# The head of a one-core attention and MLP block: x0 in two halves on two queues, another order of loads and products

## The chip, the cores and the metric

The kernel runs on one core of a Trainium2 chip. The time is device microseconds of one execution on that core; the median of three runs stands for a kernel. TensorE (PE) multiplies, VectorE (DVE), ScalarE (ACT) and GpSimd (POOL) work on its results, and SyncE (SP), ScalarE and GpSimd issue transfers.

## The reference

```python
xn = _layernorm(x, axis=-1)          # x: 1 x 2048 x 640, bf16
# A: linear attention, 32 heads of 20
q, k, v = split(xn @ wqkv)
pq, pk = phi(q), phi(k)              # phi(t) = (t + 1 if t > 0 else exp(t)) + 1e-6
kv = einsum("bhsd,bhse->bhde", pk, v)
z = einsum("bhsd->bhd", pk)
s = (pq @ kv / (pq . z + 1e-6)) @ wo
# B: MLP, 640 -> 1728 -> 640
g = silu(relu(xn @ w1) @ w2)
return x + s * g
```

## The kernel before, in words

The 2048 rows are 16 tiles of 128 rows (x0 to x15), four tiles to a chunk of 512 columns when turned. The columns of x, 640, are five blocks of 128.

The head: tiles of x are loaded (`x_load`), their means and variances taken (`bn`, `aggr`, `mean_act` on ScalarE, `half_mean_dve`), and the first four tiles are centred (`centre`), turned on PE (`head_turn`, the products on `ident` of L706), copied out of PSUM by VectorE or ScalarE (`xcT_copy`, L716 and L718), and multiplied with the key weight `wk` (`K_mm`, L733; `wk_load`, L585). Tiles are also normalised (`LN_norm`, L673) and turned a second way, by transposing transfers on SP's queue (`xnT_dma`, L722), for everything else. `fill(n)` (L605) issues idle products into a PSUM bank that nobody reads; `fill(32)` is eight of 512 columns.

The rest: the first MLP product, the query product and the others are units of seven products instead of eight on 2x2 blocks. `a0.s5` is step 5 of the first such unit of the MLP (`h_unit`, products at L1164), `p`, `q`, `k`, `m` and `g` are other families, `u` the second MLP product and `o` the attention's output. The operands of steps 5, 6, 7 and 4 are sums and differences of blocks, made on VectorE by `tt` (L936). The sums of the first chunks are `T0` (function `h_T`): number 1 (into `regE`), 3, 2 (into `regX`), 4 and 5. A step is a word of the string `PROGRAM`. `w1_load` (L582) brings 256 columns of w1, `w2_load` (L1059 and L1064) pieces of w2, `wo_load` (L1513) those of wo. `wv0`, `wv1` load the value weight (L567, on ScalarE's queue), `kv0`, `kv1` are its products (L1603), `W0` to `W5` join them with wo (L1629) and store the pieces (L1644). The denominators go out (`do`, L915) and come back spread (`rc`, L924) for the divisions (`dv`, L929). Last come `e`, `f` and `l`, the pieces of the last tiles.

The order is set by `Sched.place`: the words are recorded as operations in the order of `PROGRAM`. PE and SP keep that order always; the other engines keep it up to the word `|` (end of the head) and after it take, among the next 60 operations whose inputs are ready in a model of the times, the one with the earliest due time. The model's costs (`cost`, and in `_record` for transfers) decide only orders. Buffers hold more than one thing in turn, so loads wait until the former reader is done: w2 stands where w1 was, the value weight where scratch values of the units were.

Of the kernel before, what the change touches and what calls it, by code (L numbers as in the profile page):

```python
# [343 lines left out]


PROGRAM = """
lx0 lx2 ax1 ba0 mh0 ma0 lk02 lx3 lk24 ce0 lx4 ma1 ce1 lx5 lk45 lx7 lw2 tr0 pf3 cd0 lx6 bb0 ma2 sq1
ce2 cd1 ma3 tr1 k001 lw5 cd2 k012 ba3 lw3 ca3 mh3 ag0 ce3 S4 tr2 k102 S5 ca4 k023 k123 k134 ca5 k201
lw0 N1 tr3 N4 sq2 k213 S7 ca6 k035 ca7 k145 N5 ke0 k235 S6 bb3 N7 ag3 k301 k312 kr0 ke1 kr1 F1
N6 k325 ke2 P4 N0 kr2 P11 P5 F0 ke3 P10 KT5 kr3 KT4 N2 N3 |  # L350
SH0_1 F2 lx8 lq SH0_2 F3 lw6 wb KT7 KT6 xb wa SQ S8 xa n8 H110 n12 F6 H14 a0.s1 rb n11 F7
SM F4 SH0_3 xc T0 SH0_4 n13 H15 SK a0.s5 a0.s6 a0.s2 n9 H111 a0.s7 p1.s1 a0.s3 p1.s5 a0.s4 SH1 p1.s6 n10 n14 n15
y0 p1.s2 m0.s1 m0.s5 p1.s3 m0.s6 p1.s7 m0.s2 y4 y3 m0.s7 p1.s4 m0.s3 Kb8 m0.s4 a1.s5 a1.s1 F5 y2 Ka12 p0.s1 y1 p0.s5 a1.s6
a1.s2 p0.s6 a1.s7 a1.s3 y7 Ka8 a1.s4 p0.s2 a2.s5 a2.s1 y8 p0.s3 p0.s7 a2.s6 y5 y6 hh0 Ka11 T1 a2.s7 p0.s4 a2.s2 a2.s4 a2.s3
k1.s1 k1.s5 b0.s1 Kb12 b0.s5 y12 k1.s6 b0.s6 b0.s2 k1.s7 k1.s2 b0.s7 k1.s3 k1.s4 Kb15 b0.s4 q0.s1 b0.s3 y13 q0.s5 b1.s1 q0.s6 b1.s5 q0.s2
b1.s6 q0.s7 q0.s3 Kb11 q0.s4 b1.s7 k2.s5 b1.s3 k2.s1 b1.s4 y9 b1.s2 a3.s5 y11 k2.s6 a3.s1 Ka15 mv6 k2.s3 k2.s7 y14 a3.s6 a3.s2 k2.s4
y15 k2.s2 y10 a3.s7 q1.s5 q1.s1 a3.s3 w2a a3.s4 q1.s6 GS0 q1.s2 b2.s5 zm b2.s1 q1.s7 q1.s3 b2.s6 b2.s2 q1.s4 b2.s7 SH2 zs c0
b2.s4 m1.s1 GT1 b2.s3 GT2 m1.s5 b3.s1 m1.s6 m1.s2 b3.s5 b3.s6 m1.s7 m1.s3 b3.s2 ZS b3.s7 b3.s3 m1.s4 c1 b5.s1 b3.s4 b5.s5 b4.s5 b5.s6
b4.s1 b5.s2 b5.s7 sl b4.s6 b5.s3 zc w2b b5.s4 b4.s7 b4.s3 g0.s1 g0.s5 b4.s4 g0.s6 b4.s2 GT3 w2c dn hh1 w2d GT4 wo g0.s3
GS1 g1.s1 do0 g1.s5 g0.s2 g1.s6 g0.s7 rc0 g1.s7 do1 g1.s2 dv0 g1.s3 g1.s4 wv1 uSa0 uT1 g0.s4 uT3 wv0 uT2 uSb0 u0.s1 u0.s5  # L360
kv1 do2 kv0 rc1 W5 u0.s6 uT4 W4 u0.s2 W1 u0.s7 uSa1 W3 u0.s3 uSa2 uSb2 W0 u1.s1 u0.s4 W2 uSb1 u1.s5 u1.s6 u2.s5
u2.s1 u1.s2 u1.s7 oT u2.s6 u1.s3 u1.s4 oS0 u2.s2 xre o0.s1 u2.s7 uSa4 o0.s5 o0.s6 u2.s3 do3 u2.s4 o0.s7 o0.s2 oS1 o0.s3 uSa3 u4.s1
uSb3 dv1 uSb4 u4.s5 u4.s6 u4.s2 o0.s4 u4.s7 o1.s5 o1.s1 u4.s3 u4.s4 uSa6 rc2 o1.s6 u3.s5 oS2 u3.s1 o1.s2 o1.s7 rc3 dv2 o1.s3 u3.s6
uSb6 o1.s4 u3.s2 o2.s1 oS3 u3.s7 uSa5 o2.s5 o2.s6 u3.s3 u3.s4 o2.s2 o2.s3 o2.s7 oS4 u5.s1 u5.s5 o2.s4 u5.s6 o3.s1 u5.s2 o3.s5 uSb5 o3.s6
u5.s7 u5.s3 o3.s2 o3.s7 o3.s3 u5.s4 dv3 o3.s4 o4.s5 e3 o4.s1 u6.s1 u6.s5 o4.s6 u6.s6 uSa7 o4.s2 o4.s7 o4.s3 oS6 u6.s7 o4.s4 u6.s3 o5.s1
oS5 o5.s5 u6.s4 o6.s5 o5.s6 u6.s2 o6.s1 o5.s2 o5.s7 o5.s3 e0 uSb7 o5.s4 o6.s6 u7.s5 u7.s1 o6.s7 o6.s2 o6.s3 u7.s6 u7.s2 f0 o6.s4 u7.s7
u7.s3 f3 e1 f1 u7.s4 l0 l1
"""


def bass_recurrent_scan__linear_attn_block__dense_activation_relu__prompt_kernel(
# [187 lines left out]

    def x_load(t, n=1, E="SP", extra=()):  # L560
        sl = xs(t)
        dma(E, lambda eng: eng.dma_start(xin[:, sl:sl + n, :],
                                         x2[P * t:P * (t + n), :].rearrange("(t p) n -> p t n", p=P)),
            W=[("xin", sl + i) for i in range(n)], extra=extra)
# [106 lines left out]
    def LN_norm(t):  # L671
        mean, key = (msum[:, t, 1:2], ("msum", t, 1)) if t in BY_ACT else (mv[:, t, 0:1], ("mv", t))
        norms.append(sc.op("DVE", lambda eng: eng.tensor_scalar(  # L673
            out=xn[:, t, :], in0=xin[:, xs(t), :], scalar1=mean, scalar2=rsy[:, t:t + 1],
            op0=ALU.subtract, op1=ALU.mult), R=[("xin", xs(t)), key, ("rsy", t)], W=[("xn", t)]))
# [7 lines left out]
    def mean_act(t, lo):  # L683
        junk = ek[:, eks(t), 0, 0:D - lo]
        sc.op("ACT", lambda eng: eng.activation(out=junk, in_=xin[:, xs(t), lo:D], func=ACTF.Copy, scale=1.0 / D,
                                                accum_out=msum[:, t, 1:2]),
              R=[("xin", xs(t))], W=[("msum", t, 1), ("ek_e", eks(t))])
        sc.allow_unread.add(("ek_e", eks(t)))

    def centre(t):  # L690
        split = ((0, P * TS), (P * TS, D)) if t == 0 else ((0, D),)
        for part, (c0, c1) in enumerate(split):
# [5 lines left out]
            else:  # L698
                sc.op("DVE", lambda eng, c0=c0, c1=c1: eng.tensor_scalar(
                    out=xn[:, t, c0:c1], in0=xin[:, t, c0:c1], scalar1=msum[:, t, 0:1], scalar2=msum[:, t, 1:2],  # L700
                    op0=ALU.subtract, op1=ALU.subtract), R=[("xin", t), ("msum", t, 0), ("msum", t, 1)], W=[key])
# [1280 lines left out]
```

## Time and profile before

| | |
|---|---|
| runs | 202.53, 202.6, 204.0 us; median 202.6 |
| profiled execution | 202.56 us, span 201.3 us |
| PE | busy 197.2 us, 1312 products |
| DVE, ACT, POOL | busy 173.2, 132.5, 37.7 us |
| HBM read, written | 15.81 MB, 5.24 MB |

The span runs from the first to the last instruction that the profiler recorded; 1.26 us of the execution lie around it. A row of the timeline gives start, duration, engine, line, operation, output and inputs, count, and in brackets the idle time before it with what ended it. Modelled ends of products overlap, so that a group's length is a little over its count times the pitch. Line numbers are those of the kernel before; the changed one has them 6 or 7 higher.

### The profile page before, as it was taken

Reading aid. Unit: us, or ns where it says so; the run is one execution under the profiler, and the core shown is the slowest. Engines: PE = TensorE matmul, PEld = TensorE weight load, DVE = VectorE, ACT = ScalarE, POOL = GpSimd, SP = SyncE. Lnnn points to the kernel's source line nnn. Section 1 sums busy time; section 2 is a strip of 40 time slices with the busy share of each in tenths; the row PEclk is TensorE's granted clock in tenths of the full one; section 3 lists DMA queues with packets and bytes.
Section 4 is the critical chain, followed back from the end, with each engine's and each line's share of the span. In section 5 each row is a group of like instructions: output and inputs, shape, how many; then the busy total and the mean of one; then the engine's idle time right before and its main releaser. Section 6 shows DMA issues by size and latency. Waiting matters only on the chain.

```text
span 201.3 us, 3641 instructions
## 1 busy us (share of the span) xinstructions
PE 197.2 (98%) x1312; PEld 120.1 (60%) x1312; DVE 173.2 (86%) x407; ACT 132.5 (66%) x280; POOL 37.7 (19%) x66
## 2 busy tenths in 40 slices
...
PEclk9999999999999999999999999999999999999999
...
GB/s 179 335 259 95 150 351 144 70 98 109 108 145 134 150 256 174 171 99 67 113 17 118 270 264 184 295 212 148 355 185 72 258 65 36 33 67 65 36 65 98
DMA packets 38455, 30.43 MB, mean 151 GB/s; under 512 B 13733, under 2 KB 38437, under 8 KB 38437
## 3 DMA queue, kind: packets, MB, share of 16 engines
...
q8 instruction: 10, 0.16, 0.4%
q14 instruction: 8, 0.07, 0.1%
HBM read 15.81 MB, written 5.24 MB: 105 GB/s over the span
## 4 chain that ended last, share of the span: by engine, by line
PE 90%; DVE 4%; DMA 2%; ACT 1%; issue 1%; DVEq 0%
PE psT L991 43%; PE psT L1164 32%; PE psT L733 6%; PE psT L1494 2%; PE psT L823 2%; DMA reg<-reg 1%; ACT regE L743 1%; PE psT L1838 1%; DMA reg<-in_A_x_dram 1%; PE psT L841 1%; PE psT L1629 1%; PE psT L1603 1%; DVE stats L637 1%; DVE regX L936 1%; PE psT L895 1%
## 5 line engine op out<-in xcount | busy, mean ns | idle before, releaser
L1164 PE MATMUL psT<-reg 128*128 128x512 bf16 (+2 forms) x166 | 45.0, 370 | 0.0
L991 PE MATMUL psT<-reg,regH 128*128 128x320 bf16 (+1 forms) x224 | 35.0, 299 | 0.0
L991 PE MATMUL psT<-reg 128*128 128x320 bf16 (+1 forms) x178 | 28.4, 299 | 0.0
L991 PEld LDWEIGHTS psT<-reg,regH 128*128 128x128 bf16 (+1 forms) x224 | 21.9, 98 | 8.5
L1164 PEld LDWEIGHTS psT<-reg 128*128 128x128 bf16 (+1 forms) x166 | 15.9, 98 | 16.9 <-DVE regH L1217 0.6
L863 POOL DMA_DIRECT2D regH<-reg x16 | 18.6, 1188 | 20.9 <-DMA regH<-reg 9.4
L991 PEld LDWEIGHTS psT<-reg 128*128 128x128 f16 (+1 forms) x178 | 17.3, 98 | 7.4 <-DVE regE L899 0.4
L936 DVE TENSOR_TENSOR reg<-reg 128x1024 f16<-128x1024 bf16 (+11 forms) x30 | 19.0, 646 | 2.2 <-PE psT L991 1.8
L998 ACT ACTIVATE reg<-psT 128x320 f32<-128x320 f32 (+1 forms) x24 | 10.5, 436 | 15.8 <-PE psT L991 14.8
L1214 ACT ACTIVATE regH<-psT 128x512 bf16<-128x512 f32 (+1 forms) x24 | 14.6, 612 | 5.8 <-PE psT L1164 5.3
L1665 ACT ACTIVATE wv_sb<-psT 128x320 bf16<-128x320 f32 (+2 forms) x23 | 9.6, 424 | 11.4 <-PE psT L991 11.0
L991 PE MATMUL psT<-reg,pqT 128*128 128x320 bf16 (+1 forms) x84 | 15.8, 299 | 0.0
L936 DVE TENSOR_TENSOR psT<-psT,reg 128x320 f32<-128x320 f32 (+1 forms) x21 | 11.4, 543 | 2.8 <-PE psT L991 2.8
L637 DVE BATCH_NORM_STATS2 stats<-reg 128x6 f32<-128x320 bf16 x28 | 12.3, 480 | 1.4 <-DMA reg<-in_A_x_dram 1.1
L1853 ACT ACTIVATE reg<-psT 128x640 bf16<-128x640 f32 (+1 forms) x14 | 8.0, 570 | 7.5 <-PE psT L991 7.5
L733 PE MATMUL psT<-reg 128*128 128x320 bf16 x80 | 12.3, 299 | 0.0
L936 DVE TENSOR_TENSOR reg<-psT,reg 128x320 bf16<-128x320 f32 (+1 forms) x16 | 7.8, 489 | 5.1 <-PE psT L991 5.1
L1171 ACT ACTIVATE psT<-psT 128x512 f32<-128x512 f32 (+1 forms) x18 | 10.6, 594 | 1.8 <-PE psT L1164 1.7
L800 ACT ACTIVATE regE<-psT 128x512 bf16<-128x512 f32 x16 | 9.5, 603 | 2.6 <-PE psT L1164 2.5
L998 ACT ACTIVATE psT<-psT 128x320 f32<-128x320 f32 x17 | 7.2, 425 | 5.6 <-PE psT L991 5.5
L936 DVE TENSOR_TENSOR reg<-reg,wv_sb 128x640 bf16<-128x640 bf16 (+1 forms) x15 | 6.8, 456 | 4.3 <-ACT reg L1853 3.5
L733 PEld LDWEIGHTS psT<-reg 128*128 128x128 bf16 x80 | 7.7, 98 | 4.5 <-issue 0.4
...
## 6 DMA issues: line engine op xcount, KB each, us to landing
regH<-reg POOLq DMA_DIRECT2D x16, 320.0 KB, 3.8
reg<-in_B_w_dram SPq DMA_DIRECT2D x12, 320.0 KB, 4.9
scr<-rden SPq DMA_DIRECT2D x4, 640.0 KB, 7.0
reg<-in_A_x_dram SPq DMA_DIRECT2D x4, 640.0 KB, 6.1
...
regE<-scr SPq DMA_DIRECT2D x3, 640.0 KB, 6.1
reg<-in_A_x_dram SPq DMA_DIRECT2D x4, 320.0 KB, 4.8
...
```

The costliest lines, as they stand in the source:

```text
L637: sc.op("DVE", lambda eng: eng.bn_stats(stats[:, t, a, :], xv[:, HN * a:HN * (a + 1)]), R=[("xin", xs(t))], W=[("stats", t, a)])
L733: fns.append(lambda eng, a=a, k=k, lhs=lhs: eng.matmul(ps[bk[a]][:, 0:HN], lhsT=lhs, rhs=wk[:, k, HN * a:HN * (a + 1)], start=(k == 0), st ...
L800: exps.append(sc.op("ACT", lambda eng: eng.activation(out=e_, in_=src, func=ACTF.Exp), R=[key], W=[("er_e", es)]))
L863: dma("POOL", lambda eng: eng.dma_start(zacc[a], src, **kw), R=[key] + after, W=[("zacc", a)], chain=zchain[a])
L936: sc.op("DVE", lambda eng: eng.tensor_tensor(out=out, in0=in0, in1=in1, op=op), R=R, W=W, extra=extra)
L991: sc.group("PE", [(lambda eng, k=k, lhs=lhs, rhs=rhs: eng.matmul(ps[b][:, 0:HN], lhsT=lhs, rhs=rhs, start=(start and k == 0), stop=(k == n ...
L998: sc.op("ACT", lambda eng: eng.activation(out=dst, in_=ps[b][:, 0:HN], func=ACTF.Copy), R=[("ps", b)], W=[dkey], extra=extra)
L1164: sc.group("PE", [(lambda eng, k=k, lhs=lhs, rhs=rhs: eng.matmul(ps[b][:, 0:nn], lhsT=lhs if tile is None else rhs, rhs=rhs if tile is Non ...
L1171: sc.op("ACT", lambda eng: eng.activation(out=dst[:, 0:nn], in_=ps[b][:, 0:nn], func=ACTF.Copy), R=[("ps", b)], W=[dkey], extra=extra)
L1214: sc.op("ACT", lambda eng: eng.activation(out=dst, in_=ps[b], func=ACTF.Relu), R=[("ps", b)], W=[("hT", j, f)], extra=ex)
L1665: sc.op("ACT", lambda eng, lo=lo, hi=hi: eng.activation(out=g[:, lo:hi], in_=src[:, lo - HN * n:hi - HN * n], func=ACTF.Silu), R=[key, ("s ...
L1853: sc.op("ACT", lambda eng: eng.activation(out=o_[:, 0:n].rearrange("p (a n) -> p a n", a=2) if n == D else o_[:, 0:n], in_=src, func=ACTF. ...
```

## The change

x0 comes as two transfers of 128x320, the left half by SP's queue and the right half by ScalarE's; whoever reads the right half or the whole tile waits for both. x1 and x2 both come by ScalarE's queue (before: x1 alone). The key weight comes in five pieces of one block each, the first two directly behind x0 on SP's queue. `fill(29)` is seven idle products of 512 columns and one of 128. Five w1 pieces instead of four stand ahead of the transposing transfers on SP's queue (`wa` is the one that moved). The transposing transfers go in the order of tiles 1, 5, 4, 7, 6, 2, 0, 3; before 1, 4, 5, 7, 6, 0, 2, 3. The string `PROGRAM` is new from end to end; two constants of the model of transfers are edited.

```diff
 # Sched._record: model of a transfer
+            if names[1] == "in_A_x_dram" and size < 1e5:
+                lag, o.occ = -0.4, 0.1 if E == "ACT" else 0.5
 # Sched.place
-        lags = [(4.1, 0.6), (18.2, 1.2)]
+        lags = [(5.6, 0.6), (18.2, 1.2)]
 # PROGRAM, its first line
-lx0 lx2 ax1 ba0 mh0 ma0 lk02 lx3 lk24 ce0 lx4 ma1 ce1 lx5 lk45 lx7 lw2 tr0 pf3 cd0 lx6 bb0 ma2 sq1
+lx0 ba0 ax1 ax2 ma0 ma1 mh0 lk01 ce0 lk12 bb0 ma2 lx3 lk23 lk45 lk34 lx5 lx4 lx6 lw5 lx7 ce1 ag0 tr0
...
 # x_load
+        if t == 0:
+            for a, (Eh, key) in enumerate((("SP", ("xin", 0)), ("ACT", ("xin", 0, 1)))):
+                dma(Eh, lambda eng, a=a: eng.dma_start(xin[:, 0, HN * a:HN * (a + 1)], x2[0:P, HN * a:HN * (a + 1)]), W=[key])
+            return
...
-    fill(32)
+    fill(29)
...
 # bn, LN_norm, mean_act and centre: reads of x0's right half
-              R=[("xin", xs(t))], W=[("stats", t, a)])
+              R=[("xin", xs(t))] + ([("xin", 0, 1)] if t == 0 and a == 1 else []), W=[("stats", t, a)])
...
-              R=[("xin", xs(t))], W=[("msum", t, 1), ("ek_e", eks(t))])
+              R=[("xin", 0, 1) if t == 0 else ("xin", xs(t))], W=[("msum", t, 1), ("ek_e", eks(t))])
```

SP's queue from its start to the transposing transfers, before and after (`in_A_x` is x, `in_A_wqkv` the key weight here, `in_B_w` w1):

```order
L562 DMA reg<-in_A_x_dram 128x640 x2
L586 DMA reg<-in_A_wqkv_dram 128x2x640
L562 DMA reg<-in_A_x_dram 128x640
L586 DMA reg<-in_A_wqkv_dram 128x2x640
L562 DMA reg<-in_A_x_dram 128x640 x2
L586 DMA reg<-in_A_wqkv_dram 128x640
L562 DMA reg<-in_A_x_dram 128x640
L582 DMA reg<-in_B_w_dram 128x5x256
L562 DMA reg<-in_A_x_dram 128x640
L582 DMA reg<-in_B_w_dram 128x5x256 x3
L722 DMA_TRANSPOSE reg<-reg 128x5x128 x8
```

```order
L566 DMA reg<-in_A_x_dram 128x320
L592 DMA reg<-in_A_wqkv_dram 128x640 x2
L568 DMA reg<-in_A_x_dram 128x640
L592 DMA reg<-in_A_wqkv_dram 128x640 x3
L568 DMA reg<-in_A_x_dram 128x640 x3
L588 DMA reg<-in_B_w_dram 128x5x256
L568 DMA reg<-in_A_x_dram 128x640
L588 DMA reg<-in_B_w_dram 128x5x256 x4
L729 DMA_TRANSPOSE reg<-reg 128x5x128 x8
```

Half of x0 and x2 left this queue; the weight's first two pieces moved up behind x0, and a fifth w1 piece stands ahead of the transposing transfers.

PE and then VectorE at the first unit of the MLP, before (four fences: PE before, PE after, VectorE before, VectorE after; regE,pqT is step 5, regX,pqT step 6, regX,reg step 7, L823 and L830 plain MLP products; on VectorE, 128x1024 are the sums T0):

```order
L823 MATMUL psT<-reg 128x512 x10
L1164 MATMUL psT<-reg 128x512 x2
L823 MATMUL psT<-reg 128x512 x5
L1164 MATMUL psT<-regE,pqT 128x512 x2
L1164 MATMUL psT<-regX,pqT 128x512 x2
L1164 MATMUL psT<-reg 128x512 x3
L823 MATMUL psT<-reg 128x512 x5
L1164 MATMUL psT<-regX,reg 128x512 x2
```

```order
L830 MATMUL psT<-reg 128x512 x10
L1171 MATMUL psT<-reg 128x512 x2
L1171 MATMUL psT<-regE,pqT 128x512 x2
L830 MATMUL psT<-reg 128x512 x5
L1171 MATMUL psT<-regX,pqT 128x512 x2
L830 MATMUL psT<-reg 128x512 x5
L1171 MATMUL psT<-reg 128x512 x3
L1171 MATMUL psT<-regX,reg 128x512 x2
```

```order
L936 TENSOR_TENSOR regH<-reg 128x512
L936 TENSOR_TENSOR regX<-reg 128x1024
L936 TENSOR_TENSOR regE<-reg 128x1024
L936 TENSOR_TENSOR regX<-regX,reg 128x1024
L936 TENSOR_TENSOR reg<-reg 128x512
L759 TENSOR_SCALAR regE<-regE 128x640
L936 TENSOR_TENSOR regE<-reg,regX 128x1024
```

```order
L943 TENSOR_TENSOR regE<-reg 128x1024
L943 TENSOR_TENSOR regX<-reg 128x1024
L766 TENSOR_SCALAR regE<-regE 128x640
L943 TENSOR_TENSOR regX<-regX,reg 128x1024
L768 TENSOR_TENSOR reg<-regE 128x640
L943 TENSOR_TENSOR regE<-reg,regX 128x1024
```

Step 5 moved ahead of a group of plain products on PE, and the sum into regE that it needs moved to the front on VectorE.

SP's queue in the body, from w2 to the first load of x for the end (`rden` and `scr` are the denominators, L1644 and L1651 the stores of W), before and after:

```order
L1059 DMA reg<-in_B_w_dram 128x2x640 x6
L1059 DMA reg<-in_B_w_dram 128x640
L1064 DMA reg<-in_B_w_dram 64x640 x2
L1513 DMA reg<-in_A_wo_dram 128x640 x6
L915 DMA scr<-rden 640x1x512
L924 DMA reg<-scr 128x5x512
L915 DMA scr<-rden 640x1x512 x2
L924 DMA regE<-scr 128x5x512
L1644 DMA reg<-reg 40x640
```

```order
L1066 DMA reg<-in_B_w_dram 128x2x640 x2
L1520 DMA reg<-in_A_wo_dram 128x640 x6
L1066 DMA reg<-in_B_w_dram 128x640
L1071 DMA reg<-in_B_w_dram 64x640 x2
L1066 DMA reg<-in_B_w_dram 128x2x640 x4
L922 DMA scr<-rden 640x1x512
L931 DMA reg<-scr 128x5x512
L922 DMA scr<-rden 640x1x512
L1651 DMA reg<-reg 40x640
...
L1651 DMA reg<-reg 120x640
L931 DMA regE<-scr 128x5x512
```

Four of the w2 pieces moved behind wo, and the load of the second spread denominators moved behind the ten stores of W.

More of the change, by code (lines that the diff above doesn't have):

```diff
@@ L353 @@
[L353 to L364, printed above, removed]
@@ new lines @@
+ca5 k123 ce3 S5 k201 k035 tr3 ca6 N1 S4 N5 ca7 k213 ke0 k235 k135 k301 kr0 ke2 S7 ke1 k314 N4 S6
+k345 N7 ag3 kr1 P10 N6 N2 N0 P4 P11 N3 lq lx8 kr2 lw6 xb SH0_1 F1 ke3 kr3 |
+xa P5 KT5 wb S8 F2 F0 SH0_3 n8 F3 KT4 KT7 SH0_2 n12 SQ SK KT6 H111 rb H110 n11 a0.s1 F7 xc
+T0 F4 n10 F5 SM a0.s5 n9 n13 H14 F6 a0.s6 SH0_4 n15 n14 y6 H15 a0.s2 y0 a0.s7 p1.s1 a0.s3 T1 p1.s5 SH1
+a0.s4 p1.s6 p1.s2 y4 m0.s1 m0.s5 p1.s3 m0.s6 p1.s7 y2 m0.s2 m0.s7 y3 p1.s4 m0.s3 y7 Kb8 m0.s4 a1.s5 a1.s1 Ka12 p0.s1 y5 p0.s5
+a1.s6 y1 a1.s2 p0.s6 a1.s7 a1.s3 Ka8 a1.s4 p0.s2 y8 p0.s7 a2.s1 ZS a2.s5 hh0 a2.s6 Kb11 p0.s3 a2.s7 p0.s4 a2.s3 a2.s4 a2.s2 b0.s1
@@ new lines @@
+b0.s5 k1.s1 k1.s5 Kb12 y12 k1.s6 b0.s6 b0.s2 k1.s7 k1.s3 b0.s7 k1.s2 k1.s4 b0.s3 y13 b0.s4 q0.s1 q0.s5 Kb15 b1.s1 q0.s6 b1.s5 q0.s2 y9
+b1.s6 q0.s7 q0.s3 Ka11 y11 q0.s4 b1.s7 b1.s3 k2.s5 k2.s1 b1.s4 b1.s2 k2.s6 Ka15 a3.s1 a3.s5 k2.s7 k2.s2 a3.s6 y15 k2.s3 k2.s4 y14 a3.s2
+y10 GS0 a3.s7 q1.s5 q1.s1 a3.s3 a3.s4 GT3 q1.s6 q1.s2 zm b2.s5 GT1 b2.s1 GT2 q1.s7 q1.s3 b2.s6 b2.s2 q1.s4 b2.s7 SH2 zs c0
+b2.s4 m1.s1 b2.s3 m1.s5 b3.s1 m1.s6 b3.s5 m1.s2 b3.s6 m1.s3 m1.s7 c1 m1.s4 b3.s7 b3.s3 b5.s1 b5.s5 b3.s4 b5.s6 b3.s2 b4.s5 b4.s1 b5.s7 b5.s3
@@ new lines @@
+zc b4.s6 b5.s4 b5.s2 b4.s7 b4.s2 g0.s1 w2b b4.s4 b4.s3 wo g0.s5 g0.s6 g0.s2 hh1 dn w2d GT4 w2c g0.s3 w2a GS1 sl g1.s5
+g1.s1 uT1 g0.s7 do0 rc0 g1.s6 g1.s2 g1.s7 uT3 do1 g0.s4 uSa0 uT2 g1.s3 mv6 g1.s4 wv0 wv1 uSb0 u0.s1 kv1 u0.s5 uT4 kv0
+dv0 uSa1 W5 W4 uSb1 u0.s6 u0.s2 W3 uSa2 W1 u0.s3 W2 u0.s7 u1.s1 u1.s5 u0.s4 W0 u1.s6 oT u2.s1 uSb2 u2.s5 oS0 u1.s3
+u1.s7 u2.s6 u1.s2 u1.s4 uSa3 u2.s7 oS1 u2.s3 rc1 o0.s1 o0.s5 uSb3 uSa4 u2.s2 xre o0.s6 u2.s4 o0.s2 o0.s7 o0.s3 u4.s1 u4.s5 dv1 o0.s4
+u4.s6 oS2 uSb4 o1.s5 u4.s2 o1.s1 u4.s7 u4.s3 o1.s6 u4.s4 o1.s2 do3 do2 o1.s7 o1.s3 u3.s1 o1.s4 rc3 u3.s5 u3.s6 uSa5 u3.s2 o2.s1 oS3
@@ L368 @@
+o2.s5 rc2 uSa6 u3.s7 o2.s6 u3.s3 dv2 uSb5 u3.s4 o2.s2 o2.s3 o2.s7 u5.s1 u5.s5 o2.s4 dv3 o3.s5 u5.s6 o3.s1 u5.s2 o3.s6 o3.s2 u5.s7 o3.s7
+uSb6 u5.s3 o3.s3 o3.s4 oS4 u5.s4 u6.s5 uSa7 oS5 o4.s1 u6.s1 o4.s5 o4.s6 o4.s2 u6.s6 o4.s7 o4.s3 u6.s7 o4.s4 oS6 o5.s5 u6.s3 o5.s1 u6.s2
+u6.s4 o5.s6 e3 o5.s2 o6.s1 o5.s7 o5.s3 o6.s5 o6.s2 o6.s6 o5.s4 u7.s5 u7.s1 uSb7 o6.s7 e0 u7.s6 o6.s3 u7.s2 o6.s4 f0 u7.s7 e1 f3
+u7.s3 f1 u7.s4 l0 l1
 """
```

14 lines of the change are left out of this document (4 added, 10 removed).

## The prediction

> **What bounds the kernel now.** I read the page's head first, then TensorE's waits and its timeline to 29 us, then the queues that feed it.
>
> ```profile
> span 201.3 us, 3641 instructions
> PE 197.2 (98%) x1312; PEld 120.1 (60%) x1312; DVE 173.2 (86%) x407; ACT 132.5 (66%) x280; POOL 37.7 (19%) x66
> PEclk9999999999999999999999999999999999999999
> ```
>
> ```profile
> PE psT L733 <- DVE regX L716: 0.6, 1, 0.6
> PE psT L1164 <- DVE psT L936: 0.2, 1, 0.2
> ```
>
> TensorE (PE) is busy 197.2 of 201.3 us, at full granted clock in every slice. In the whole program its waits for another engine's data are two, in the columns total, times, longest: 0.6 us before the first key product (L733) and 0.2 us at a product of the first h_units (L1164). The change leaves its real products the same in number and width, so what it can win lies ahead of the last of these waits, and every microsecond of a new wait behind it counts whole.
>
> ```profile
> 0.83 3.38 PE L605 MATMUL psT<-const-bfloat16-1.0 128*128 128x512 bf16 x8 [0.83 <-PEq L1967]
> 4.34 0.63 PE L706 MATMUL psT<-ident,reg 128*128 128x128 bf16 x5
> ...
> 6.04 0.70 PE L733 MATMUL psT<-reg,regX 128*128 128x320 bf16 x4 [0.63 <-DVE regX L716]
> 12.03 4.48 PE L823 MATMUL psT<-regX,reg 128*128 128x512 bf16 x20
> ...
> 23.94 0.59 PE L1164 MATMUL psT<-reg 128*128 128x512 bf16 x2
> 25.45 0.59 PE L1164 MATMUL psT<-regE,pqT 128*128 128x512 f16 x2
> 28.58 0.60 PE L1164 MATMUL psT<-regX,reg 128*128 128x512 f16 x2 [0.17 <-DVE psT L936]
> ```
>
> Until 6.04 PE waits for data: eight idle products, the transposes of x0 at 4.34, keys from 6.04. From there to 198.7 it is packed but for a few tenths near 26 and 28.6. A product 512 wide costs 4.48/20, some 0.22 us; an idle one 3.38/8 = 0.42.
>
> **The start.** What sets 4.34 and 6.04:
>
> ```profile
> 0.79 2.34 DMA reg<-in_A_x_dram
> ...
> 3.93 0.64 DVE reg L699 x2
> ```
>
> ```profile
> 4.78 0.28 DVE L716 COPY regX<-psT 128x256 bf16<-128x256 bf16 x1
> ```
>
> ```profile
> 1.71 0.43 SPq L586 DMA_DIRECT2D reg<-in_A_wqkv_dram  x1
> ```
>
> ```profile
> reg<-in_A_wqkv_dram SPq DMA_DIRECT2D x1, 320.0 KB, 4.2
> ```
>
> ```profile
> 0.96 0.39 ACTq L562 DMA_DIRECT2D reg<-in_A_x_dram  x1
> ```
>
> x0 is issued at 0.79 and lands 2.34 later, at 3.13; statistics and half mean end at 3.9, the centring starts at 3.93, the transposes 0.41 behind it. The first key product needs x0's turned columns, copied by 5.06, and the first two chunks of the key weight, issued at 1.71 and landed 4.2 later: 5.91. So 6.04 is set by the weight, though the row of waits names the copy. The second row of that transfer decides, since the copy had been done for a microsecond.
>
> After: SP issues half of x0 (0.4 us) and then weight chunks 0 and 1 singly, at about 1.2 and 1.65; ScalarE's queue takes the other half and x1, x2, at 0.39 us an issue. Half a load moves half the bytes. The two ends for its landing: 2.34 as for the whole tile, or 2.34 less half the tile's time on the engines. For that time:
>
> ```profile
> 2.50:3.25 0.75, 0.75 (x3) 0.29 (x2) 0.10 (x1) 0.10 (x1) 0.07 (x1) 1.00 1.00 348
> 3.50:4.75 1.25, 1.11 (x7) 0.24 (x5) 1.18 (x5) 1.25 (x5) 0.00 (x0) 1.00 0.86 235
> ```
>
> The last column is GB/s. With two queues feeding (2.50 to 3.25) the engines moved 348, with SP's alone (3.50 to 4.75) 235. A tile of 164 KB takes 0.47 to 0.70 us, half of it 0.24 to 0.35. So the centring starts between 3.55 and 3.93; I take 3.75, since half the chain (statistics of the second half, ScalarE's mean) waits for the later half, on the queue that carries x1 too. Chunk 0 is half of the old 320 KB piece, issued 0.5 earlier: it lands between 4.8 and 5.6, chunk 1 between 5.3 and 5.9. Now the copies rule as much as the weight: two centrings ahead of the copy, 0.85 + 0.28 behind 3.75, then 0.3 for those of x1. First key product: 5.25 to 6.0, taken as 5.5. The keys run behind the next tiles' transposes too, so not all of the 0.54 survives; end of the first keys and start of the H products 11.6, against 12.03, with 11.3 and 12.1 as ends. I book **0.4 us of gain**, 0 to 0.75.
>
> The Trainium skill, DMA: Bandwidth & Descriptors, section Rules for kernel authors, speaks against the halves: spreading loads over SP, ScalarE and GpSimd brings no bandwidth, as all run on the same 16 engines, and saves only issue time. The two rows above disagree for the stretch in which SP alone kept the engines 0.86 busy and two queues 1.00; by the page the halves would bring nothing and the start would be won by the weight's place alone, the second rival below.
>
> Idle products: three quarter-pieces fewer, 0.32 us less of work whose end (4.2 in the row) PE must pass before it turns x0. With the centring at 3.75 the transposes are due at 4.15; the idle ones end by 3.9. They cost nothing unless the clock rises later for it. Idle products at 0.42 and real ones at 0.22 show that it rises near 4 us, on work that now ends there. If it rose one such stretch (3.4 us) later, the some 2 us of real products in that stretch would take twice as long: a rival with its own price.
>
> **The transposing transfers and the first h_units.**
>
> ```profile
> 6.19 3.30 SPq L582 DMA_DIRECT2D reg<-in_B_w_dram  x3
> 10.17 12.16 SPq L722 DMA_TRANSPOSE reg<-reg  x8
> ```
>
> ```profile
> L722 SPq DMA_TRANSPOSE reg<-reg x8: 1265/1276/2614, 10.2 to 21.1; - x8
> ```
>
> ```profile
> reg<-reg SPq DMA_TRANSPOSE x1, 2.6
> ```
>
> ```profile
> 9.74 0.40 DVE L673 TENSOR_SCALAR reg<-reg,msum,rsy 128x640 bf16<-128x640 bf16 x1
> ...
> 23.72 0.43 DVE L936 TENSOR_TENSOR regH<-reg 128x512 f16<-128x512 bf16 x1 [0.45 <-DMA reg<-reg]
> 24.06 0.68 DVE L936 TENSOR_TENSOR regX<-reg 128x1024 f16<-128x1024 bf16 x1
> 24.66 0.69 DVE L936 TENSOR_TENSOR regE<-reg 128x1024 f16<-128x1024 bf16 x1
> ```
>
> SP issues the eight transposing transfers from 10.17 in one row, 1.28 each with one of 2.61, and the last (issued 21.05) lands 2.6 later: 23.69. VectorE's first sum of four tiles waits for that and starts at 23.72, the first product pair on plain operands at 23.94. Call the last landing L. The set of tiles is the same and the row of eight as long, so L moves with the start of the row and with where the slow one falls.
>
> The start of the row: SP's last w1 issue ended at 9.49 (6.19 + 3.30), and the row began at 10.17 because tile 1 was normalised at 9.74 + 0.40 on VectorE. One w1 load more now stands ahead, and two issues for the weight; x2 and half of x0 left SP (0.4 to 0.5 each). Tile 1's statistics move up with the rest of the start, some 0.5. If SP's issues are the limit, it is free at 9.49 plus one or two issues of 0.45, about 10; if the engines are, 320 KB more take 0.95 to 1.4 us at the rates above, and 9.49 becomes 10.9. The ends are 9.6 and 11.2; I take 10.3, the middle of the two readings less what the two queues gain early. L = 23.69 + 0.13: 23.1 to 24.8, taken 23.8.
>
> Behind L the order on VectorE changes: the sum that the pair at 25.45 needs (regE, 0.60 pitch) stood third, behind 0.34 + 0.60, and stands first. So this pair may start at L + 0.8 = 24.6 and PE runs its three pieces of H work later. Between it and the pair now at 28.58 lie 17 products of 0.216: 3.67. With L = 23.8, 24.6 + 3.67 = 28.27, against 28.58: 0.3 of gain if the start has arrived there too (H ends 0.4 earlier, and PE's own work up to a0.s1 then has 0.4 us to wait for L, so the start's gain and this one are **one gain and not two**). Taken 0.3, ends -0.7 (L 24.8) and +0.75. Tile 5's keys follow the 20 H products, now at 15.9; its transfer moves from third to second in the row, 1.28 earlier, so it isn't late unless the row starts 0.9 later. What reaches the body is **0.3 us**.
>
> **The body.** A PE packed for 170 us can lose only where something comes late. Two places look tight; both are on queues the new order rearranged.
>
> ```profile
> 70.85 40.29 SPq L1059 DMA_DIRECT2D reg<-in_B_w_dram  x7
> ```
>
> ```profile
> 114.82 1.33 DVE L936 TENSOR_TENSOR reg<-reg 128x2240 f16<-128x2240 bf16 x1 [0.39 <-DMA reg<-in_B_w_dram]
> ...
> 117.97 0.49 DVE L936 TENSOR_TENSOR reg<-psT,wv_sb 128x320 bf16<-128x320 f32 x1
> ```
>
> ```profile
> 118.49 0.38 ACTq L567 DMA_DIRECT2D wv_sb<-in_A_wqkv_dram  x1
> ```
>
> ```profile
> wv_sb<-in_A_wqkv_dram ACTq DMA_DIRECT2D x1, 320.0 KB, 4.0
> ```
>
> ```profile
> 124.55 1.60 PE L1603 MATMUL psT<-reg,wv_sb 128*128 128x120 bf16 x30
> ```
>
> ```profile
> 128.25 0.38 SPq L924 DMA_DIRECT2D regE<-scr  x1
> 128.68 8.85 SPq L1644 DMA_DIRECT2D reg<-reg  x10
> ```
>
> ```profile
> regE<-scr SPq DMA_DIRECT2D x1, 640.0 KB, 6.2
> ```
>
> ```profile
> 137.66 0.69 DVE L929 TENSOR_TENSOR pqT<-pqT,regE 128x1024 bf16<-128x1024 bf16 x1
> ```
>
> First: the sum at 114.82 waited for the last w2 load (landed 114.8). Two of the w2 loads were issued from 70.85 on and now stand last of all nine, behind the six of wo. Two pieces of 320 KB more in the final burst are 1.9 to 2.8 us at the rates above, so the last landing comes at 116.7 to 117.6. Behind this sum on VectorE stands the addition that frees the value weight's buffer (117.97), so the load of 118.49 goes out 1.3 + 0.5 behind that landing, 118.5 to 119.4, and lands 4.0 later, 122.5 to 123.4. The products that need it are due earlier, right behind u0.s1, at some 123.5 rather than 124.55. That hides it, by 0.1 to 1.0. Taken 0, ends 0 and 0.4 (the last piece half a microsecond slower). Queued behind late value products are W's, whose copies then come late too.
>
> Second: the reciprocal of the denominators for the second quarter was issued at 128.25 and used by VectorE at 137.66, 3 us behind its landing. It now stands behind the ten W stores, which end at 137.5: issued between 135.7 and 137.5 and landing 6.2 later: 143.7 at the worst, 142 if the stores go earlier. Division dv1 stands behind u4.s5 in the new order, near 143.5 to 144. VectorE runs in order, so a late landing holds the sums that PE needs about 2 us behind; taken 0, ends 0 and 0.8. Cost booked for both, for ordinary friction of another order: **0.05**.
>
> The tail keeps its steps (last W, e and f pieces, l0, l1), so nothing there.
>
> **The sum.** Profiled execution 202.56 (span 201.3 and 1.26 around it), the median of the three is 202.6: the same within 0.04. 202.56 - 0.3 + 0.05 = **202.3**. The likeliest's own range, from the start's gain of 0.75 at L 23.1 to no gain, is 201.8 to 202.7.
>
> **Rivals.**
> (a) The transposing row is pushed back by the fifth w1 load: if the engines are the limit (they were full, share 1.00, in the row from 2.50), the row starts at 11.2 and L is 24.8; pair at 25.6, last of its products at 29.3, 0.7 later than 28.58: 203.2, slower than before. It decides from L over 24.1 (24.1 + 0.8 + 3.67 = 28.57). For it: three loads took 3.30 us to issue. Against: two x tiles leave SP.
> (b) Halves no earlier, each 2.34 behind its issue: centring 3.93, keys 5.7, 0.1 won in the end: 202.5. For it: the 2.34 is five times the 0.47 that the tile's bytes take at 348 GB/s, so most of it need not shrink with the bytes.
> (c) The value weight behind w2's last load, or dv1 behind the reciprocal: worst ends 0.4 and 0.8 with the gain kept, 202.56 - 0.3 + 0.4 to 0.8 = 202.7 to 203.1.
> (d) The clock rises late: 2 us of products twice as long, less the 0.6 PE waits there anyway: 202.56 + 1.4 - 0.3 = 203.7.
> (e) All ends good, start 5.25 and the row at 9.6: 202.56 - 0.75 = 201.8. No case reaches 200.5: the wait of 0.6, that of 0.2 and the 0.4 by which x0 may be centred earlier are 1.2 together.
>
> The Trainium skill, TensorE: Matmul & The Clock Gate, Part 1, has a rule for (d): the clock opens after about 3.4 us of activity seen by a free-running window, so that the count of slow products varies from run to run. By that rule, 3.38 us of idle work cut to 3.1 may fall short in some runs. The trace of before shows only that 3.38 sufficed.
>
> **Chances.** Forecast 0.46, (a) 0.15, (b) 0.16, (c) 0.12, (d) 0.05, (e) 0.06. A measurement of this kernel tells about 1% (2 us) from no change. Faster by over 1% needs 2 us, more than the first 6 us have to give: 0.02. Slower by over 1% needs (d) with (a), or a stall in the body that I don't see, though a new order has many such places: 0.08. Within: 0.90. The range that leaves out 2 in 10: 201.7, just under (e), to 203.4, over (a) and (c).
>
> **What would show it.** Right: x0's transposes at 4.1 to 4.2, first key product 5.3 to 5.7, H products from 11.6, transposing row at 10.3 with the last landing at 23.8, the regE,pqT pair 0.8 behind it, and no wait of PE over 0.2 us after 30. Wrong: the row at 11 or later, a new PE wait at the value products (L1603 of before) or near 145, idle-rate products after 4.2. Should the time be under 201 or over 204, the packed body was not packed as I read it.

## The result and the profile after

| | before | changed |
|---|---|---|
| median, 14 runs each | 202.66 us | 204.54 us |
| lowest and highest | 202.14, 204.0 | 203.31, 210.77 |
| profiled execution | 202.56 | 203.31 |
| span | 201.3 | 201.9 |

The ratio of the changed kernel to the one before is 1.0081, interval [1.0056, 1.0106]: slower, by some 1.6 us. It was forecast at 202.3, with a range from 201.7 to 203.4. The ratio leaves out the changed kernel's two runs over 208 us (209.91 and 210.77). Note that the profiled execution is the fastest of the 14: what its trace shows is the least of the loss.

From the profile page of the changed kernel:

```profile
span 201.9 us, 3630 instructions
PE 196.8 (97%) x1302; PEld 120.1 (59%) x1312; DVE 171.6 (85%) x408; ACT 132.4 (66%) x279; POOL 36.2 (18%) x66
```

The same products (ten of the 1312 records are missing in this trace), and three waits of 1.3 us together (total, times, longest), all ahead of 25 us, where there were two of 0.8 together. These 0.5 us are nearly all of the 0.6 by which the span grew:

```profile
PE psT L713 <- DVE reg L701: 0.9, 1, 0.9
...
PE psT L713 <- DVE reg L705: 0.2, 1, 0.2
PE psT L1171 <- issue: 0.2, 1, 0.2
```

PE's timeline of the changed kernel, the answer to the rows from 0.83 to 28.58 of before:

```profile
0.83 3.25 PE L611 MATMUL psT<-const-bfloat16-1.0 128*128 128x512 bf16 x8 [0.83 <-PEq L1974]
4.33 0.70 PE L713 MATMUL psT<-ident,reg 128*128 128x128 bf16 x5 [0.25 <-DVE reg L705]
...
6.13 0.45 PE L713 MATMUL psT<-ident,reg 128*128 128x128 bf16 x5 [0.95 <-DVE reg L701]
6.42 0.71 PE L740 MATMUL psT<-reg,regX 128*128 128x320 bf16 x4
...
25.41 0.60 PE L1171 MATMUL psT<-regE,pqT 128*128 128x512 f16 x2
...
29.09 0.59 PE L1171 MATMUL psT<-regX,reg 128*128 128x512 f16 x2
```

Of before, the row of x1's transposes and the landing of x1's transfer:

```profile
4.97 0.44 PE L706 MATMUL psT<-ident,reg 128*128 128x128 bf16 x5
```

```profile
reg<-in_A_x_dram ACTq DMA_DIRECT2D x1, 160.0 KB, 2.6
```

x0 is turned at 4.33 (before 4.34), so the halves brought nothing. x1 is turned at 6.13 instead of 4.97, and the first key product follows at 6.42 instead of 6.04. Step 7 of the first unit is at 29.09 instead of 28.58. What x1 waited for stands in the chain of waits:

```profile
1.39 3.42 DMA reg<-in_A_x_dram
4.81 0.02 issue
4.83 0.84 ACT regE L691 x2
5.67 0.02 issue
5.69 0.40 DVE reg L701
```

x1's transfer, now second on ScalarE's queue behind the half of x0, was issued at 1.39 instead of 0.96 and took 3.42 us instead of 2.6 (two pieces of the key weight from SP's queue were in flight): 4.81 instead of 3.6, then its mean and its centring.

The transposing transfers start at 10.59 (before 10.17), and the last, issued at 21.35, takes 3.2 (2.6): 24.6, against 23.7. VectorE's first sum follows at 24.66:

```profile
6.57 3.98 SPq L588 DMA_DIRECT2D reg<-in_B_w_dram  x4
10.59 12.04 SPq L729 DMA_TRANSPOSE reg<-reg  x8
```

```profile
reg<-reg SPq DMA_TRANSPOSE x1, 3.2
```

```profile
24.66 0.69 DVE L943 TENSOR_TENSOR regE<-reg 128x1024 f16<-128x1024 bf16 x1 [1.00 <-DVE pqT L943]
```

In the body, the rows that answer to 114.82, 117.97, 118.49 and 124.55 of before (VectorE, ScalarE's queue, PE):

```profile
119.16 1.33 DVE L943 TENSOR_TENSOR reg<-reg 128x2240 f16<-128x2240 bf16 x1 [0.59 <-DMA reg<-in_B_w_dram]
120.41 0.48 DVE L943 TENSOR_TENSOR reg<-psT,wv_sb 128x320 bf16<-128x320 f32 x1
```

```profile
120.92 0.38 ACTq L573 DMA_DIRECT2D wv_sb<-in_A_wqkv_dram  x1
```

```profile
124.25 0.81 PE L1610 MATMUL psT<-reg,wv_sb 128*128 128x120 bf16 x15
```

The last w2 piece lands at 119.1 instead of 114.8, the value weight's load goes out at 120.92, lands 3.0 later at 123.9, and PE takes it at 124.25. In this run, 0.34 us were to spare. Before, it was 2.1.

### The profile page after: what moved, and what is told of

The parts are those of the page before. It is cut to its first block, busy times and chain, and to the rows that moved or that the text cites. A ratio compares the mean times of both kernels' runs of the same rounds, so it can differ in the third digit from the quotient of the medians.

```text
span 201.9 us, 3630 instructions
## 1 busy us (share of the span) xinstructions
PE 196.8 (97%) x1302; PEld 120.1 (59%) x1312; DVE 171.6 (85%) x408; ACT 132.4 (66%) x279; POOL 36.2 (18%) x66
## 4 chain that ended last, share of the span: by engine, by line
PE 86%; DVE 7%; DMA 3%; ACT 1%; issue 1%; DVEq 0%
PE psT L998 42%; PE psT L1171 30%; PE psT L740 5%; PE psT L1501 2%; DMA reg<-in_A_x_dram 2%; PE psT L830 2%; PE psT L1845 1%; PE psT L848 1%; DMA reg<-reg 1%; DVE reg L768 1%; DVE regX L943 1%; DVE regH L943 1%; DVE stats L643 1%; PE psT L1636 1%; PE psT L1610 1%
## 5 line engine op out<-in xcount | busy, mean ns | idle before, releaser
L1171 PE MATMUL psT<-reg 128*128 128x512 bf16 (+2 forms) x161 | 43.6, 370 | 0.4 <-issue 0.2
L998 PE MATMUL psT<-reg 128*128 128x320 bf16 (+1 forms) x178 | 29.2, 299 | 0.0
L943 DVE TENSOR_TENSOR reg<-psT,reg 128x320 f32<-128x320 f32 (+2 forms) x20 | 10.0, 505 | 5.0 <-PE psT L998 5.0
L998 PEld LDWEIGHTS psT<-reg,pqT 128*128 128x128 bf16 (+1 forms) x84 | 8.2, 98 | 3.2
```

Source lines behind the costliest of these rows:

```text
L943: sc.op("DVE", lambda eng: eng.tensor_tensor(out=out, in0=in0, in1=in1, op=op), R=R, W=W, extra=extra)
L998: sc.group("PE", [(lambda eng, k=k, lhs=lhs, rhs=rhs: eng.matmul(ps[b][:, 0:HN], lhsT=lhs, rhs=rhs, start=(start and k == 0), stop=(k == n ...
L1171: sc.group("PE", [(lambda eng, k=k, lhs=lhs, rhs=rhs: eng.matmul(ps[b][:, 0:nn], lhsT=lhs if tile is None else rhs, rhs=rhs if tile is Non ...
```

## The experiments

Theory: what the best run does not show is waiting at the value products, with a little at the head. Rival: all of it is made at the head.

### The changed kernel again, and the two halves of the order

`c1_repeat` is unedited.

> The changed kernel again, nothing edited, to see a second profile of it and its spread. Theory: the time above the best run is waiting at two places of the body, the value products behind the last w2 landing (0.34 us of room in the first profile) and the second division behind its reciprocals (0.4 us of room). A run that is slower than 203.3 should show PE idle just ahead of the value products (L1610) or near 144 to 147. About 204.2. Rival: the spread is made in the first 30 us (landing of x1 and of the last transposing transfer), and PE is packed behind 30 in every profile. Second rival: products are slower, PE's pitch above 0.136 for 320 columns.

203.63 to 209.52 us, median 205.55. The profiled execution has a span of 208.1; its waits and PE's timeline:

```profile
PE psT L1610 <- issue: 2.3, 1, 2.3
PE psT L713 <- DVE reg L701: 0.9, 1, 0.9
```

```profile
6.74 1.27 PE L740 MATMUL psT<-reg,regX 128*128 128x320 bf16 x4
...
14.47 0.81 PE L830 MATMUL psT<-regX,reg 128*128 128x512 bf16 x3
```

The theory's wait is there, and 2.3 us long. But the head has something that neither theory had: four key products take 1.27 us here and 0.71 in the first profile. PE ran at half rate until near 9.8, and the plain products began at 14.47 instead of 12.63. The windows of the same trace (us, busy time with counts for PE, PEld, DVE, ACT and POOL, then granted clock, DMA share, GB/s) show that the wait at the value products costs a second time:

```profile
122.00:126.50 4.50, 4.50 (x34) 3.04 (x32) 4.05 (x5) 1.20 (x3) 0.00 (x0) 1.00 0.54 106
126.50:129.00 2.50, 0.19 (x4) 0.17 (x4) 2.45 (x3) 0.42 (x1) 0.00 (x0) 1.00 0.87 268
129.00:132.40 3.40, 3.40 (x32) 2.60 (x31) 1.58 (x4) 0.44 (x1) 0.00 (x0) 0.54 0.74 260
132.40:135.80 3.40, 3.40 (x30) 2.60 (x29) 2.60 (x4) 1.00 (x2) 0.00 (x0) 0.95 0.04 13
```

PE stood for 2.3 of 2.5 us, and the 3.4 us behind it ran at 0.54 of the clock: 1.6 us more. With the 2.6 us by which step 7 of the first unit is late (31.21 against 28.58), that makes 6.5 of the 6.8 us by which this span of 208.1 is longer than the one before, so this run of 209.52 us is long by the kernel's own waits. The other four runs of the changed kernel over 208 us left no trace, and whether they have the same cause is not shown.

`c2_headnew_bodyold` and `c3_headold_bodynew` join the orders at a point near 72 us at which both kernels have done the same steps.

```diff
-PROGRAM = changed order
+PROGRAM = changed order up to Ka15 a3.s1 a3.s5 | order of before from there   # c2
+PROGRAM = order of before up to Ka15 | changed order from there              # c3
```

> The changed kernel's order up to some 72 us (its loads, halves, 29 idle pieces, first units), and from there the order of before. Theory (body waits): the head costs 0.5 (first key product 6.4 against 6.0, last products of the first unit at 29.1 against 28.6), the rest nothing: 203.1, with as little spread as before. Rival (all in the head): 204.0 to 204.5 and the spread of the changed kernel.

> The converse: the kernel before up to some 72 us, and from there the changed order. Theory (body waits): the value products come up to 0.5 earlier and wait more, so nothing of the head's gain is kept: 203.5 to 204.2, spread 1.5 us or more, with a PE wait at the value products of 0.2 us or more. Rival (all in the head): 202.6.

c2: 204.53, ratio 1.0079 [1.0048, 1.0110]. c3: 203.9, ratio 1.0062 [1.0040, 1.0084]. The body alone loses 1.3 us, so the rival (all in the head) is out. But the head's half alone loses as much as the whole change, 1.4 us more than my theory gave it; the two losses do not add. c2's profiled run had half-rate keys as c1 and one wait of 0.6 us near 95 that neither parent has, so that part of its loss may come from the joining. c3 lost as said, but 3 us further on: W's products waited for VectorE, which had its four long w2 sums late:

```profile
114.25 4.50 DMA reg<-in_B_w_dram
118.76 0.02 issue
118.78 2.96 DVE reg L935 x3
...
127.27 0.45 PE psT L1628 x2
```

### The w2 loads

```diff
-... w2d GT4 w2c g0.s3 w2a ...
+... w2c w2a w2d GT4 g0.s3 ...            # c4_w2d_last
-a3.s3 a3.s4 ... w2a GS1
+a3.s3 w2a a3.s4 ... GS1                  # f2_w2a_early
```

> The changed kernel with two words moved: the loads w2c and w2a ahead of w2d, whose gate (111.5 in the profile) holds four pieces of 320 KB behind it. Theory: the last w2 landing comes at 115 to 117 instead of 119.1, the value weight's load goes out 2 us earlier, the value products never wait; what is left is the head and the division: 203.3 to 203.6, less spread. Rival (all in the head): 204.2 as the changed kernel.

205.32 to 212.89, median 209.19: a miss, and the other way. The four pieces of 320 KB now went out ahead, from 112.32, but the fourth landed only near 120, and the small ones, now behind them, at 120.9. The body ran some 1.5 us later here (wo issued at 107.86 instead of 106.34); even so the large pieces came no earlier, so their place behind the small ones is not the whole of the late landing. The new order let two long sums pass ahead of the addition that frees the value weight's buffer:

```profile
120.97 2.56 DVE L943 TENSOR_TENSOR reg<-reg 128x2240 f16<-128x2240 bf16 x2 [0.88 <-DMA reg<-in_B_w_dram]
123.44 0.48 DVE L943 TENSOR_TENSOR reg<-psT,wv_sb 128x320 bf16<-128x320 f32 x1
```

```profile
wv_sb<-in_A_wqkv_dram ACTq DMA_DIRECT2D x1, 320.0 KB, 7.4
```

```profile
131.43 1.32 PE L1610 MATMUL psT<-reg,wv_sb 128*128 128x120 bf16 x15 [5.24 <-issue]
```

The load left at 123.96, behind two transfers of denominators of 640 KB (123.14 and 123.56), and took 7.4 us. In the profiles of the changed kernel and its other versions where it left half a microsecond or more ahead of both, it took 3.0 to 3.6, and in c1, where it left 0.14 us ahead of the first, 4.6. So the price of being late isn't proportional: in this one trace, half a microsecond past the denominators went with four more. (With the order of loads of before, the same load took 3.6 to 5.7 us ahead of them, so its length varies for other reasons too.)

> The changed kernel with one word, w2a, put back to where it stood before, behind a3.s3, so that two pieces of 320 KB load some 40 us earlier and the last burst has five pieces instead of seven. Theory: last w2 landing 1.6 to 2 us earlier (117.5 to 118.5, with the head as late as its clock makes it), value weight landed before PE needs it, no PE wait at the value products: 203.2 to 203.8, and no run above 206. Rival (other waits take its place, as when w2d went last): no change, 204.2.

The wait at the value products is gone: no PE wait over 0.2 us behind 30, and no run above 206. The last w2 piece landed by 117.6 instead of 119.1, as forecast. But the value weight's load did not leave earlier for it: it left at 121.27 (120.92 in the first profile), because VectorE now took two of the long sums ahead of the addition, and it landed 0.3 us ahead of PE, as in the first profile. So the early landing is shown, and that it removed the wait is not. The profiled run has 203.83, but the median of six is 204.61, ratio 1.0090, above the theory.

`f1_before_neww2` puts the changed order of w2 and wo alone into the kernel before.

> The kernel before with the changed kernel's order of loads in the body alone: wo ahead, then the three small w2 pieces, then the four of 320 KB, none of them early. Theory (the last w2 landing gates the value weight's load through VectorE's order): last landing at 118.5 to 120, the value weight issued at 120.5 to 122, PE waiting 0.2 to 1.0 us at or just behind the value products: 203.0 to 204.0. Rival (the body's loss is the changed order of PE and VectorE, not the loads): 202.5.

203.36, ratio 1.0024 [0.9996, 1.0052]: 0.5 to 0.8 us, in the range of the theory, though the interval still includes no change. The order of loads by itself puts the last w2 landing at 119.9 (before 114.8), as the theory said. The path from there was another, so the time was met by luck: VectorE's order had moved, the value weight's load left at 118.20, ahead of that landing, and PE's wait, 0.4 us just ahead of the value products, is for a VectorE sum that stood behind the long w2 sums.

### The key products at half rate

> The changed kernel with fill(32) as before, nothing else. In three of four profiles with the new head the key products ran at half rate (474 ns for 320 columns instead of 299) until about 9.8, which puts the first H product at 14.4 to 14.8 instead of 12.6. Theory: it is the pause of PE between the transposes of x0 and of x1 (5.1 to 6.1, x1 landing late) that keeps the clock down, so three quarter pieces more, 0.13 us of filled time before 4.2, change little: 204 to 205, cold key products again. Rival: the missing idle products keep it down, so key products at 299 ns from the first and 202.5 to 203.3.

> The kernel before with fill(29). Theory (the pause decides): x1 is early there, the key products stay at full rate, 202.5, the same as before. Rival (the idle products decide): cold key products in most runs, 203.5 to 204.5.

`fill(32)` in the changed kernel: 204.28, ratio 1.0080 [1.0063, 1.0096]. Its profile has the first four key products in 0.71 us, full rate, as the rival said, but the time is the theory's. `fill(29)` in the kernel before: 202.51, ratio 1.0007 [0.9989, 1.0026], full rate too. So fewer idle products by themselves bring neither half rate nor loss. Whether they help it on where x1 is late is not settled: the one profile with `fill(32)` and a late x1 ran at full rate, and so did four of the eight with `fill(29)`.

```diff
-lw2 ca1 sq1 pf3 ma3
+lw2 ca1 sq1 pf10 ma3                                             # d2_pf10
-            for a, (Eh, key) in enumerate((("SP", ("xin", 0)), ("ACT", ("xin", 0, 1)))): ...
+            dma("SP", lambda eng: eng.dma_start(xin[:, 0, :], x2[0:P, :]), W=[("xin", 0), ("xin", 0, 1)])   # d3_x0whole
```

> The changed kernel with the idle products behind the first transposes made 10 quarter pieces instead of 3, which fills PE from 4.8 to 6.0, just the pause in which it waits for x1. Theory (the pause keeps the clock down): key products at 299 ns from the first or second group, first H product 12.6 to 13.0, 203.0 to 203.8, what is left being the body's waits. Rival (the first idle products decide, or chance): cold as often as the changed kernel, 204 to 205.

> The changed kernel with x0 as one transfer on SP's queue, so that x1 is the first on ScalarE's and x2 the second. Theory: x1 lands near 3.6 instead of 4.8, its transposes start at 5.3 instead of 6.1, the pause is 0.2 to 0.4 us and the clock is up by 6.2; x0 centred at 3.9 as before: first H product 12.0 to 12.6, 203.0 to 203.6. Rival (weight pieces on SP's queue delay x1 whatever its place): x1 at 4.5 or later, no change.

d2: 204.38, ratio 1.0094; d3: 204.24, ratio 1.0082. Both profiles have key products at full rate (d3: x1 landed at 3.7, first key product at 5.78, plain products from 11.99, as early as before), and neither is faster in the median; both are above their theories. PE waited 0.7 and 0.6 us at the value products, in d2 also 0.5 for x1 near 6.5, in d3 also 0.3 for a transposing transfer near 20.6. In d3 the head's gain went into these two waits. d3 also shows that the weight pieces on SP's queue do not delay x1 whatever its place, as its rival had it: they stand there as in the changed kernel.

`f3_w2a_x0whole` has x0 in one transfer and w2a early together. Expected were 202.8 to 203.3, and 203.7 or more if the rest of the new order loses by itself. It took 204.13, ratio 1.0066 [1.0053, 1.0078], the rival's range. The first key product came at 5.68 and nothing waited at the value products, but two waits for transposing transfers, at 16.86 and 21.62, took the gain:

```profile
PE psT L739 <- DMA reg<-reg: 1.2, 2, 0.7
```

That the pause brings the half rate is best seen in `i1`, below. There the clock had risen by 3.7, x1 came late, and the windows read:

```profile
0.80:3.50 2.70, 2.67 (x7) 1.01 (x8) 1.64 (x4) 1.84 (x3) 1.39 (x6) 1.00 0.55 149
3.50:6.90 3.40, 1.82 (x17) 0.93 (x15) 2.10 (x9) 2.19 (x8) 0.45 (x2) 1.00 1.04 360
6.90:10.30 3.40, 3.40 (x18) 2.11 (x16) 3.37 (x13) 2.25 (x7) 2.34 (x6) 0.50 1.06 317
10.30:13.70 3.40, 3.40 (x30) 2.52 (x28) 3.32 (x10) 2.50 (x5) 2.30 (x5) 1.00 1.32 255
```

PE was busy for 1.82 of 3.40 us, and the next 3.40 ran at 0.50 although PE never paused in them. Finer windows of the same trace put the fall near 6.9 (0.71 of the clock in 6.80 to 7.00) and the rise near 10.3 (0.63 in 10.00 to 10.40). Of the nine profiles with x1 late, four have such a stretch (c1, c2, c4, i1), which cost 1.4 to 1.7 us each; of the ten with x1 on time, five of them with `fill(29)`, none has. In c1, c2 and c4 the rate had not yet risen when the pause came. The Trainium skill, TensorE: Matmul & The Clock Gate, Part 1, says that a free-running window of some 3.4 us of activity sets the rate; these rows agree, in length (3.40 us) and in that the half rate behind a pause does not come in every run (four of nine). In the four profiles the half rate ended between 9.8 and 10.3, and in c1 it came once more at 129. PE need not stand for a whole window: 1.58 us of 3.40 were enough in i1.

### The fifth w1 piece, and all together

```diff
-ma3 cd0 ce2 sq2 wa tr1 ... lw6 xb SH0_1
+ma3 cd0 ce2 sq2 tr1 ... lw6 xb wa SH0_1      # h1_wa_back, and h2 with x0 whole and w2a early
```

> The changed kernel with one word, wa (the fifth w1 piece), put back behind the transposing transfers, where it stood before. In the profiles of the changed head with full clock the last transposing transfer lands at 24.6 to 24.9 instead of 23.7 and PE waits 0.25 to 0.8 us for one of them near 21. Theory (the fifth piece loads the transfer engines while the row runs): last landing 23.4 to 24.0, no wait near 21, 0.4 to 0.8 us less: 203.3 to 203.8, the value products still waiting. Rival (the late x1 moves everything behind it): last landing 24.5 or later, 204.2.

> The changed kernel with three words or lines put back: x0 in one transfer, wa behind the transposing transfers, w2a early; the new order of products and the new place of the key weight stay. Theory (these three are the causes): 202.4 to 202.9, the same as before within what can be told. Rival (the new order loses by itself): 203.5 or more.

h1: the last transposing transfer landed at 23.0 instead of 24.6 and no wait stood near 21, as the theory said; the time is 204.18, ratio 1.0078, unchanged: x1's pauses (1.1 us together) and the value products (0.4) ate it, and step 7 of the first unit came at 29.25 all the same. i1, below, has the landing at 23.3; with x0 in one transfer it came at 24.2 with the fifth piece moved (h2, i2) as without (d3), so the piece is not all that sets it. h2: 205.01, ratio 1.0121, which proves nothing, since VectorE's order had moved and PE waited 1.2 us for the first sum. The order there follows from modelled times, so an edit of a load re-sorts an engine that it doesn't touch. `g1_before_ax2` fell into the same hole:

> The kernel before with x2 on ScalarE's queue behind x1 and the key weight's first 320 KB right behind x0, no other edit: the part of the change that the runs so far speak for. First key product 5.6 to 5.9 instead of 6.0 to 6.4. Theory (what bounds the head is the row of transposing transfers and VectorE's sums behind it): 202.3 to 202.6, no gain that can be told. Rival (the start is worth its length): 202.0 to 202.2.

204.0, ratio 1.0065, with 1.3 us of waiting for a VectorE sum at 29.7 that before doesn't have. So three runs had the order on VectorE, ScalarE and GpSimd written out as a list, and only the queues edited:

> The changed kernel with wa behind the transposing transfers and w2a early, on SP's queue alone; the order on VectorE, ScalarE and GpSimd is written out as the changed kernel has it, so that nothing else moves (with h2 the rows of VectorE had moved too, and PE waited 1.3 us for a sum there). x0 stays in halves, so x1 stays late. Theory: last transposing landing 23.0 to 23.7, no wait at the value products, head late by x1 alone: 203.0 to 203.5. Rival (the new order of PE and VectorE loses by itself): 203.8 or more with no single wait over 0.4 us.

> The same with x0 in one transfer as well. Theory (late x1, the fifth w1 piece and the late w2 pieces are all of the loss): 202.4 to 202.9, like the kernel before. Rival: 203.5 or more.

> The kernel before with x2 on ScalarE's queue and the key weight's first 320 KB right behind x0, the order on VectorE, ScalarE and GpSimd written out as it was (with g1 it had moved, and PE waited 1.5 us for a sum at 29.7). Theory (the row of transposing transfers bounds the head): first key product 0.1 to 0.5 earlier, and 202.3 to 202.6, no change that can be told. Rival (the start is worth its length): 202.0 to 202.2.

| kernel | median us | ratio to before |
|---|---|---|
| changed | 204.54 | 1.0081 [1.0056, 1.0106] |
| i1: wa and w2a put back | 204.58 | 1.0097 [1.0069, 1.0126] |
| i2: and x0 whole, x1 early | 203.2 | 1.0031 [1.0014, 1.0048] |
| i3: before with x2 on ScalarE's queue, key weight first | 202.71 | 1.0018 [0.9993, 1.0043] |

i1 missed its theory by more than 1 us: PE waited 1.2 us for x1, and the half rate above followed. i1 and i2 differ in x0's halves alone: 0.6%, 1.3 us. So x1's lateness, with the pauses and the half rate that it brings, is the largest piece found, but only with the other two put back; by itself (d3) putting it right gained nothing that can be told. The three together take back some 0.5% of 0.8%. i2 lies between its theory (to 202.9) and its rival (from 203.5). Its waits are few:

```profile
PE psT L729 <- DVE reg L721: 0.4, 1, 0.4
PE psT L756 <- DMA reg<-reg: 0.3, 1, 0.3
```

Its span is 201.5, 0.2 more than before, while its time is 0.5 to 0.6 more: in the mean of its runs 1.58 us lie around the span, 1.39 with the changed kernel and 1.24 with the one before. What these 0.3 and 0.15 us are, the profile doesn't show, and they stay open. i3 had its first key product at 5.79 instead of 6.04 and gained nothing, as the theory said: the first units wait for the transposing transfers and VectorE's sums all the same. No version beat the kernel before.

## Why the prediction was wrong, step by step

The step that failed first is the start: 0.4 us were booked as gain, and the first key product came 0.4 later than before, because the landing of x1 stood in no sum. Two more terms were too small: the transposing row, and the wait behind w2's last load.

- **What bounds the kernel**: right. PE is packed, and each new wait counted whole (0.5 us more of waits, 0.6 of span in the profiled execution).
- **x0 in halves**: the value taken for the centring, 3.75, was wrong; it came at 3.92. The half on SP's queue landed at 2.8, but the one on ScalarE's at 3.23, as late as the whole tile had (3.13), and the mean needs both. Rival (b) had this centring, though not the first key product that followed.
- **First key product at 5.5, ends 5.25 and 6.0**: measured 6.42, outside. This step failed by an omission. The step priced x0 and the weight and, of the things on PE ahead of the product, asked only for x0's copy. The weight was not what counted: its chunk 0 landed at 3.95, ahead of the forecast (4.8 to 5.6). On PE the transposes of x1 stand ahead of the first key product, and "0.3 for those of x1" took x1 as landed. x1 had been moved too, behind the half on its queue and against two weight pieces on the other, and I did not cost its landing: 4.81 instead of 3.6.
- **Idle products and rival (d)**: the price was near (1.4 forecast, 1.4 to 1.7 measured), the cause was not, so the nearness is luck. Fewer idle products alone do nothing (d4); x1's pause brings it, in four of nine profiles, where the chance was put at 0.05.
- **Transposing row**: 10.59 against 10.3 taken, the last landing 24.6 against 23.8, inside the ends of 23.1 and 24.8. Of the 0.9 us by which it is later than before, 0.3 are the later issue of the last transfer and 0.6 its longer way (3.2 against 2.6). Rival (a) came true at nearly its price, step 7 being 0.5 late instead of 0.3 early: its 0.8 + 3.67 behind 24.6 gives 29.07, and 29.09 was measured. It had the row itself pushed back to 11.2, which did not happen. h1 shows that the fifth w1 piece makes the landing late while x0 comes in halves; step 7 did not come earlier without it, since x1 held PE back.
- **Value weight behind w2, rival (c)**: the right place and mechanism, and the worst mis-sizing. The landing was put at 116.7 to 117.6 by bytes alone; it was 119.1. SP's rows show why:

```profile
111.46 0.33 SPq L1066 DMA_DIRECT2D reg<-in_B_w_dram  x1
111.83 1.21 SPq L1071 DMA_DIRECT2D reg<-in_B_w_dram  x2
113.08 2.12 SPq L1066 DMA_DIRECT2D reg<-in_B_w_dram  x4
```

  The small pieces, which wait until 111.46 for their place, now stand ahead of the four large ones, of which two had gone at 108.5 before. Of the 4.3 us, f2 gives 1.6 to the two pieces that moved to the end; the other 2.7, from this wait and from wo's six pieces ahead, were in no sum and are not separated (c4, with the large ones ahead, brought them no earlier). The end of 0.4 us was thus far too low: PE waits were 0.4 to 0.7 in four profiles, 2.3 and 5.2 in two, and then the clock fell as well.
- **Second reciprocals behind W's stores**: right at 0. They landed at 142.2 and were used at 142.61; no profile has a PE wait there.
- **The range**: the ends of the single steps were treated as if they came one at a time. In the profiles they came together: x1, the last transposing transfer and the last w2 piece were all late in the same run.
